# Moving pad fills from VectorE to GpSimd and GpSimd's own fills later, with new load order, tile order and PSUM rotation, in a gated mix of linear attention and a SwiGLU FFN

## The chip, the cores and the metric

The kernel runs on one core of one Trainium2 chip. The metric is the device time in microseconds (us) of a whole execution. Before the change it is 291.82 us (median of 4 runs, 291.61 to 292.34). Runs of one kernel scatter by up to 2.2 us here (291.45 to 293.68 for the kernel before on one chip; 3.0 us in e6, with one outlier), so experiments were run in five rounds beside the kernel before on the same chip, and comparisons between chips are made by the ratio to it.

Engines in the profile: PE = TensorE (matmuls), DVE = VectorE, ACT = ScalarE, POOL = GpSimd, SP = the queue that starts most DMAs; a q behind a name is the engine's own instruction queue. L330 is a line of the program, often a helper's: L340 fills, L330 `tensor_scalar`, L326 `scalar_tensor_tensor`, L322 `tensor_tensor`, L318 copies, L312 ScalarE's activations, L306 transposes, L294 matmuls. The granted clock is the share of its full clock that TensorE was given.

## The reference, cut to what matters

With S = 2048 tokens, D = 640, 32 heads of 20 and F = 1728:

```python
x = A_x
g = sigmoid((x * gate_w).sum(-1, keepdims=True))
q, k, v = split_heads(x @ A_wqkv)
# phi: softmax(+k @ w_phi) and softmax(-k @ w_phi), side by side
kv  = einsum("bhsf,bhsd->bhfd", phi_k, v);  z = phi_k.sum over tokens
a = (phi_q @ kv) / (phi_q . z + 1e-6)       # per head
b = (silu(x @ w_gate) * (x @ w_up)) @ w_down
out = g * (a @ wo) + (1 - g) * b
```

## The kernel before

The program is two lists of words. `LOADS` is the order of the DMAs, `ORDER` the order of the work items; each item sends its instructions to several engines, and every engine runs its own in that order. A helper counts who last wrote and read which bytes and places the waits. What matters here:

- `H` = two warming matmuls on ones, `X t` = transpose tile t of x on TensorE, `G` = the gate column, `U t.c` / `V t` = v projection of tile t, `M`/`R` = premultiply the k and q weights by w_phi, `K`/`S`/`P`/`E` = k tile, its sums, its normalisation on GpSimd (2.36 us each), its sum into k-v; `F b.k` = one FFN item; `Q`/`A`/`B`/`C`/`c` = the q side; `J` = the gates; `I`/`N` = begin and end of the k phase.
- PSUM is handed out in four pairs of banks. During the k phase pair 3 holds the k-v sums and the other three rotate.

```python
FCUT = [0, 384, 1024, F_FFN]                # three loads of gate/up columns
XQ = ["sp", "act", "act", "sp"]             # queues that load x0..x3
...
memset("dve", ones[:, :], 1.0)
for buf in (v1r, v1x):                      # pads of the v tiles
    v1v = buf[:, :, :].rearrange("p b (h d) -> p b h d", d=DH + 1)
    memset("dve", v1v[:, :, H, :], 0.0)
    memset("dve", v1v[:, :, :, DH:DH + 1], 1.0)
memset("dve", ekr[:, :, 1280:FK], 0.0)
memset("dve", krec[:, :, :], 0.0)
memset("pool", wog[:, :, :], 0.0)
...
memset("pool", ph[:, :, :], 0.0)            # 128 x 4224, buffers of the scaled q
...
def next_pair():
    r = ring["i"] % ring["n"]               # round robin; n is 3 in the k phase, else 4
    ring["i"] += 1
    return r
...
def kv_end():                               # N
    kv_finish()                             # VectorE: zt, zf, dz, then kvsb from banks 6 and 7
    ring["n"] = 4

def gates():                                # J, all on 128 x 16 float32
    tsc(svec[:, :], svec[:, :], 60.0, None, ALU.min, ALU.bypass)   # VectorE tensor_scalar
    actop(g2[:, :], svec[:, :], ACTF.Exp)                          # ScalarE
    tsc(omg[:, :], g2[:, :], 2.0, 2.0, ALU.mult, ALU.add)
    recip(omg[:, :], omg[:, :])
    tsc(g2[:, :], g2[:, :], 2.0, None, ALU.mult, ALU.bypass)

def fitem(bt, k):                           # F (cut)
    mm(...gate, up into the two banks of one pair...)
    actop(h, g, ACTF.Tanh, 0.5)             # ScalarE reads PSUM
    actop(u, up, ACTF.Copy)                 # ScalarE reads PSUM
    stt(h, h, 1.0, g, ALU.add, ALU.mult)    # VectorE reads PSUM: now the pair is free
    tt("pool", h, h, u, ALU.mult)           # GpSimd
```

The softmax here doesn't subtract the row's maximum and nothing guards it: scores larger than these inputs give would overflow.

## Time and profile before

| | before |
|---|---|
| span of the profiled execution | 289.8 us |
| PE busy | 285.8 us (99%) |
| DVE / ACT / POOL busy | 168.9 / 148.7 / 157.0 us |
| first useful matmul (transpose of x0) | 4.64 us |
| first gate matmul (F0.0) | 12.87 us |

The chain of waits of the kernel before (start, length, what; followed back from the last instruction) shows what bounds it:

```profile
3.66 0.33 DVE v1x L340
...
4.36 0.04 DVE wvg L318
...
4.45 0.39 PE ps L294 x2
...
11.49 276.34 PE ps L294 x1900
287.83 0.03 issue
287.86 0.32 DVE osb L697
```

After 11.49 us TensorE never stops: 1900 matmuls in one piece. The spacing is dense: a 128x512 matmul follows the last by 216 ns, from 12.87 us on, and the trace shows no closer spacing of that shape. So I saw nothing to win after the start without fewer matmuls, and much to lose: a wait put into that piece can cost up to its full length (an estimate from the piece without a stop).

The start in the timeline of before (start, length, engine, line, operation, output<-input, shapes, count; in brackets the idle time before it and what ended that):

```profile
2.85 0.82 PE L294 MATMUL ps<-ones 128*128 128x128 bf16 x6
...
3.66 0.33 DVE L340 MEMSET v1x<- 128x330 bf16 x1 [1.25 <-issue]
...
4.28 0.11 DVE L318 COPY wvg<-ps 128x5 bf16<-128x5 bf16 x1
...
4.45 0.39 PE L294 MATMUL ps<-ones 128*128 128x128 bf16 x2 [0.78 <-DVE wvg L318]
4.64 0.74 PE L306 MATMUL ps<-ident,xs 128*128 128x128 bf16 x5
```

The gate column's copy queues behind the pad fills on VectorE, and a warming matmul waits 0.78 us for its PSUM pair. That is what the change goes for.

The gates, from the same timeline:

```profile
75.05 0.17 DVE L330 TENSOR_SCALAR svec<-svec 128x16 f32<-128x16 f32 x1
75.21 1.15 POOL L322 TENSOR_TENSOR hT<-hT,us 128x512 bf16<-128x512 bf16 x1 [0.20 <-DVE svec L330]
...
75.50 0.89 DVE L330 TENSOR_SCALAR omg<-g 128x16 f32<-128x16 f32 x1 [0.28 <-ACT g L312]
...
76.59 0.11 DVE L330 TENSOR_SCALAR g<-g 128x16 f32<-128x16 f32 x1
```

Three `tensor_scalar` of the same 16 columns take 0.17, 0.89 and 0.11 us. The slow one ends at 76.39, just as GpSimd's product ends (75.21 + 1.15 = 76.36).

### The profile page before, as it was taken

The page shows a single profiled execution, that of the slowest core. Times are in us where ns is not written, and L with a number is a line of the kernel's source. Part 1 is how long each engine was busy: PE and PEld are TensorE (multiplying, and loading weights), DVE is VectorE, ACT ScalarE, POOL GpSimd, SP SyncE. Part 2 cuts the span into 40 slices and gives each one's busy share as a digit, 9 for nine tenths or more (in the row PEclk, how much of TensorE's full clock was granted, in tenths as well). Part 3 has the DMA queues.
Part 4 walks back from the last instruction along what each step waited for, and adds up shares of the span by engine and source line. Part 5 has one row for each costly group of instructions (what it writes and reads, how often), then busy time and mean ns, then how long its engine had stood idle before and what let it go on. Part 6 is the DMA issues. An engine that isn't in the chain of part 4 may idle for free.

```text
span 289.8 us, 4879 instructions
## 1 busy us (share of the span) xinstructions
PE 285.8 (99%) x1975; PEld 174.8 (60%) x1975; DVE 168.9 (58%) x248; ACT 148.7 (51%) x252; POOL 157.0 (54%) x118
## 2 busy tenths in 40 slices
PE   7999999999999999999999999999999999999997
PEld 5657777767544554447775557655444457746776
DVE  3244866768678999699998399238265337011000
ACT  1456778777465637584344743434565552172112
POOL 8731986987646786968333736411597454213000
PEclk9999999999999999999999999999999999999999
DMA  7976878000192205202362213500022003500101
GB/s 201 249 109 127 111 214 313 3 5 0 41 314 66 50 2 100 50 2 58 87 111 59 47 35 68 79 23 23 2 50 50 0 2 72 75 23 1 48 23 49
DMA packets 48777, 21.28 MB, mean 73 GB/s; under 512 B 39346, under 2 KB 48754, under 8 KB 48754
## 3 DMA queue, kind: packets, MB, share of 16 engines
q1 hardware_dynamic: 46712, 19.76, 31.1%
q10 hardware_dynamic: 2042, 1.20, 1.6%
q8 instruction: 16, 0.26, 0.4%
q14 instruction: 7, 0.06, 0.1%
HBM read 8.96 MB, written 2.62 MB: 40 GB/s over the span
## 4 chain that ended last, share of the span: by engine, by line
PE 98%; issue 1%; DVE 1%
PE ps L294 97%; PE ps L306 1%; DVE v1x L340 0%; DVE v1r L340 0%; DVE osb L697 0%; DVE krec L340 0%; DVE ones L340 0%; DVE ekr L340 0%; DVE wvg L318 0%
## 5 line engine op out<-in xcount | busy, mean ns | idle before, releaser
L322 POOL TENSOR_TENSOR hT<-hT,us 128x512 bf16<-128x512 bf16 (+1 forms) x56 | 67.5, 1215 | 67.9 <-DVE hT L326 67.7
L326 DVE SCALAR_TENSOR_TENSOR hT<-hT,ps 128x512 bf16<-128x512 bf16 (+1 forms) x56 | 37.8, 684 | 65.6 <-ACT hT L312 60.5
L294 PE MATMUL ps<-xT,wg 128*128 128x512 bf16 x260 | 64.6, 379 | 0.0
L294 PE MATMUL ps<-xT,wu 128*128 128x512 bf16 x260 | 64.6, 379 | 0.0
L294 PE MATMUL ps<-wd,hT 128*128 128x320 bf16 (+2 forms) x462 | 63.9, 295 | 0.0
L312 ACT ACTIVATE hT<-ps 128x512 bf16<-128x512 f32 (+2 forms) x60 | 35.8, 597 | 43.8 <-PE ps L294 43.6
L294 PEld LDWEIGHTS ps<-wd,hT 128*128 128x128 bf16 x462 | 44.5, 98 | 17.0
L322 POOL TENSOR_TENSOR ph<-eq,qc 128x1320 bf16<-128x1320 bf16 x16 | 40.3, 2520 | 24.8 <-DVE qc L610 15.3
L294 PE MATMUL ps<-wqk,xT 128*128 128x320 bf16 x320 | 47.7, 299 | 0.0
L312 ACT ACTIVATE osb<-ps,omg 128x640 bf16<-128x640 f32 (+2 forms) x17 | 12.9, 758 | 61.4 <-PE ps L294 61.4
L294 PEld LDWEIGHTS ps<-xT,wu 128*128 128x128 bf16 x260 | 25.4, 98 | 30.7
L322 POOL TENSOR_TENSOR ekr<-ekr,krec 128x1280 bf16<-128x1280 bf16 x16 | 37.4, 2357 | 11.5 <-DVE krec L336 9.6
L294 PEld LDWEIGHTS ps<-xT,wg 128*128 128x128 bf16 x260 | 24.9, 98 | 29.3 <-ACT oT L312 0.8
L294 PEld LDWEIGHTS ps<-wqk,xT 128*128 128x128 bf16 x320 | 30.7, 98 | 13.0 <-issue 0.4
L312 ACT ACTIVATE us<-ps 128x512 bf16<-128x512 f32 (+1 forms) x56 | 33.3, 595 | 1.3 <-POOL hT L322 1.2
L333 DVE TENSOR_REDUCE ksum<-ekr 128x64 f32<-128x1280 bf16 x16 | 23.4, 1464 | 12.4 <-ACT ekr L312 12.4
L312 ACT ACTIVATE eq<-ps 128x640 bf16<-128x640 f32 x32 | 22.4, 703 | 11.5 <-POOL ph L322 7.1
L312 ACT ACTIVATE ekr<-ps 128x640 bf16<-128x640 f32 x32 | 22.4, 704 | 7.2 <-PE ps L294 6.7
L333 DVE TENSOR_REDUCE qz<-eq 128x64 f32<-128x1280 bf16 x16 | 23.7, 1479 | 2.7 <-ACT eq L312 2.7
L294 PE MATMUL ps<-wvg,xT 128*128 128x320 bf16 (+1 forms) x160 | 25.0, 304 | 0.1
L294 PE MATMUL ps<-wog,oT 128*128 128x320 bf16 (+2 forms) x165 | 24.7, 294 | 0.0
L333 DVE TENSOR_REDUCE qw<-ez 128x64 f32<-128x1280 bf16 x16 | 23.6, 1478 | 0.1
(73 smaller groups left out, 191.6 us busy)
## 6 DMA issues: line engine op xcount, KB each, us to landing
out_dram<-osb SPq DMA_DIRECT2D x15, 160.0 KB, 1.8
wd<-in_B_w_down_dram SPq DMA_DIRECT2D x1, 2080.0 KB, 10.9
wg<-in_B_w_gate_dram SPq DMA_DIRECT2D x1, 880.0 KB, 9.8
wu<-in_B_w_up_dram SPq DMA_DIRECT2D x1, 880.0 KB, 11.5
wg<-in_B_w_gate_dram SPq DMA_DIRECT2D x1, 800.0 KB, 5.6
wu<-in_B_w_up_dram SPq DMA_DIRECT2D x1, 800.0 KB, 7.9
wog<-in_A_wo_dram SPq DMA_DIRECT2D x2, 375.0 KB, 7.5
wvg<-in_A_wqkv_dram SPq DMA_DIRECT2D x3, 160.0 KB, 4.1
```

The source lines that it names most:

```text
L294: last = pe.matmul(o, lhsT=l, rhs=r, start=st, stop=sp_, skip_group_check=sk)
L306: last = pe.transpose(o, i, ident[0:k, 0:k])
L312: return run("act", lambda: act.activation(o, i, func, scale=scale), rd, [o])
L322: return run(e, lambda: eo.tensor_tensor(o, a, b, op), [a, b], [o])
L326: return run("dve", lambda: dve.scalar_tensor_tensor(out=o, in0=a, scalar=s, in1=b, op0=op0, op1=op1), rd, [o])
L333: return run("dve", lambda: dve.tensor_reduce(o, i, AX.X, ALU.add), [i], [o])
```

## The change

The intent is to free VectorE at the start, to bring x2 and x3 sooner, to put less data ahead of the transposing DMAs, and to pick the PSUM pair whose last use lies furthest back. `LOADS` and `ORDER` are rewritten to fit.

```diff
-x0 w0 x1 w1 w2 x2 w3 w4 x3 f0 h k0 k1 t4 ...
+x0 w0 x1 w1 x2 w2 x3 w3 w4 h f0 k0 k1 t4 ...
-FCUT = [0, 384, 1024, F_FFN]
+FCUT = [0, 256, 896, F_FFN]
+XQ = ["sp", "act", "act", "act"]           (WQ alike, and the first up load on sp; cut)
 ORDER (cut to two places):
-H0 H3 H11 H8 H6 H7 H9 G H4 H5 H2 H1 X0 H10 X1 ...
+H0 H8 H6 H13 H9 H11 H5 H7 H10 G H2 H14 H12 H3 H1 X0 H4 X1 ...
-... P15 F1.6 J F0.12 E13 E14 E15 N L F0.7 ...
+... P15 i4 F1.13 F0.2 J F1.2 E12 E13 E14 E15 Q0 Q2 Q1 N F0.13 ...
+def fills(i):
+    if i < 2:      memset("pool", v pads of v1r / v1x)
+    elif i == 2:   memset("pool", ekr pads); memset("pool", krec)
+    elif i == 3:   memset("pool", wog), kvsb, eq, qc, hmask
+    else:          memset("pool", ph[:, :, :], 0.0)
+for i in range(3): fills(i)                 # i3 and i4 stand in ORDER
-ring = {"n": 4, "i": 0}
+ring = {"n": 4, "lru": [0, 1, 2, 3]}
+held = set()                                # pairs with an unfinished v tile
+def used(r): ...                            # puts pair r last in the order of use, returns it
 def next_pair():
-    r = ring["i"] % ring["n"]; ...
+    return used([r for r in ring["lru"] if r < ring["n"] and r not in held][0])
```

More of the change, by code (lines that the diff above doesn't have):

```diff
@@ L31 @@
 LOADS = """
-x0 w0 x1 w1 w2 x2 w3 w4 x3 f0 h k0 k1 t4 k2 k3 k4 t5 t6 t7 t8 t9 t10 t11 t12 t13 t14 t15 q0 q1 q2 q3
+x0 w0 x1 w1 x2 w2 x3 w3 w4 h f0 k0 k1 t4 k2 k3 k4 t5 t6 t7 t8 t9 t10 t11 t12 t13 t14 t15 q0 q1 q2 q3
 q4 f1 f2
@@ L36 @@
 ORDER = """
-H0 H3 H11 H8 H6 H7 H9 G H4 H5 H2 H1 X0 H10 X1 U0.0 U0.1 U1.0 U0.2 U1.1 X2 U1.2 U0.3 U1.3 U0.4 U2.0
-U2.1 U2.2 U1.4 X3 U2.3 U2.4 Y V3 F0.0 M0 F0.2 M1 F0.1 M3 M4 V4 M2 V5 K0 V8 S0 K1 S1 K2 K3 V7 V13
-P0 I S2 E0 K4 P1 E1 V6 S3 P2 P3 R1 S4 K5 V10 E2 K6 E3 P4 S5 E4 P5 S6 R0 K8 R3 K7 E5 P6 S7 K9 V9 S8
-E6 R4 V15 P7 S9 R2 K10 V14 E7 P8 P9 S10 K11 E8 V11 K12 P10 E9 S11 S12 P11 P12 K13 Q1 E10 K14 S13 T
-F0.3 E11 V12 A1 P13 K15 Q0 S14 S15 Q2 P14 E12 P15 F1.6 J F0.12 E13 E14 E15 N L F0.7 F1.12 F1.8 Z
-A0 B0 F0.11 C0 c0 B1 F0.13 F1.2 F0.9 F1.0 C1 F1.10 F0.5 A2 Q3 F1.13 B2 B3 c1 F0.4 Q4 A3 C2 c2
-F0.10 F1.4 C3 Q5 c3 B5 F1.11 F0.8 A5 F1.5 F0.6 F1.1 F1.7 A4 F1.9 B4 C4 c4 O0.1 Q6 O0.0 C5 c5 A6
-O0.2 F1.3 Q7 B6 B7 D0.3 A7 D0.0 Q8 C6 c6 C7 c7 Q9 A9 D0.2 Q10 B9 B8 D0.1 A8 C8 O1.0 O1.1 c8 A10 C9
-O1.2 F2.11 Q11 c9 F2.5 B10 Q12 A12 F2.6 C10 B11 F2.4 A11 F2.10 D1.1 C11 c10 Q13 B12 D1.0 A13 c11
-F2.13 B13 Q14 D1.3 F2.7 C13 F2.1 C12 D1.2 O2.2 B14 A14 O2.0 O2.1 F3.10 F3.0 c13 F3.4 F2.12 F3.13
-c12 F3.9 C14 F3.8 F2.8 F3.1 F3.7 F2.2 F3.6 F2.3 F2.9 F3.2 F2.0 F3.12 Q15 c14 A15 D2.1 B15 C15 c15
-D2.2 D2.3 O3.2 O3.1 O3.0 F3.3 F3.11 F3.5 D2.0 D3.2 D3.1 D3.0 D3.3
+H0 H8 H6 H13 H9 H11 H5 H7 H10 G H2 H14 H12 H3 H1 X0 H4 X1 U0.0 U0.1 U1.0 X2 U1.1 U0.2 U1.2 U2.0
+U2.1 X3 U2.2 U1.3 Y U2.3 U1.4 U0.3 U2.4 V3 U0.4 i3 F0.0 F0.1 M0 M1 V4 M2 M3 M4 K0 S0 K1 K3 S1 P0
+P1 K2 V5 V6 I E0 K4 S2 P2 S3 V8 E1 K5 E2 V7 K6 P3 E3 S4 S5 K7 V11 P4 P5 E4 V14 S6 P6 K8 E5 R0 S7
+K9 V9 S8 R1 P7 E6 S9 E7 P8 K10 R3 K11 P9 S10 E8 V10 V13 E9 R4 K12 S11 P10 K13 T E10 K14 S12 P11
+P12 E11 S13 V12 V15 S14 R2 K15 P14 P13 F1.10 S15 F0.11 P15 i4 F1.13 F0.2 J F1.2 E12 E13 E14 E15 Q0
+Q2 Q1 N F0.13 A0 F1.11 Z B0 F0.7 B1 F1.7 C0 c0 F0.6 F1.3 A1 A2 F0.3 L B2 C1 F0.5 Q3 c1 B3 F0.10
+F1.0 Q4 C2 c2 B4 F0.12 F1.12 F0.4 A3 F1.1 C3 Q5 B5 c3 F0.8 A5 F1.5 F1.8 F0.9 A4 F1.4 F1.9 C5 c5 C4
+O0.2 Q6 c4 O0.1 O0.0 A6 B6 Q7 Q8 C6 B7 D0.2 A7 D0.1 c6 A8 C7 c7 Q9 D0.0 A9 Q10 B8 C8 F1.6 D0.3 B9
+O1.0 O1.2 B10 C9 O1.1 F2.6 c9 c8 F2.2 D1.0 Q12 Q11 A10 C10 F2.8 c10 Q13 A11 F2.7 F2.13 A13 B11
+D1.3 C11 F2.10 c11 D1.2 F2.4 B12 B13 A12 D1.1 O2.1 O2.0 O2.2 C12 Q14 C13 F2.11 c12 F2.1 F3.6 Q15
+F2.12 F2.0 A15 F2.9 B15 c13 F2.5 F3.8 F2.3 F3.13 C15 F3.5 c15 F3.7 B14 F3.11 F3.1 F3.9 F3.12 A14
+F3.0 C14 F3.4 F3.10 D2.1 c14 F3.3 D2.3 O3.2 O3.0 O3.1 F3.2 D2.0 D2.2 D3.0 D3.1 D3.2 D3.3
 """
@@ L356, in select @@
             channel_multiplier=cm), [ap], [ap])
-    XQ = ["sp", "act", "act", "sp"]
-    WQ = ["sp", "sp", "act", "sp", "act"]
+    XQ = ["sp", "act", "act", "act"]
+    WQ = ["sp", "sp", "sp", "sp", "act"]
     x2 = A_x[0]
@@ L374, in load_ffn @@
         dma("sp", wg[:, :, c0:c1], B_w_gate[:, c0:c1].rearrange("(c p) j -> p c j", p=P))
-        dma("sp" if c0 else "act", wu[:, :, c0:c1], B_w_up[:, c0:c1].rearrange("(c p) j -> p c j", p=P))
+        dma("sp", wu[:, :, c0:c1], B_w_up[:, c0:c1].rearrange("(c p) j -> p c j", p=P))
     def load_wv(c):
@@ L402, in _build @@
     memset("dve", ones[:, :], 1.0)
-    for buf in (v1r, v1x):
-        v1v = buf[:, :, :].rearrange("p b (h d) -> p b h d", d=DH + 1)
-        memset("dve", v1v[:, :, H, :], 0.0)
-        memset("dve", v1v[:, :, :, DH:DH + 1], 1.0)
-    memset("dve", ekr[:, :, 1280:FK], 0.0)
-    memset("dve", krec[:, :, :], 0.0)
-    memset("pool", wog[:, :, :], 0.0)
-    memset("pool", kvsb[:, :, :], 0.0)
-    memset("pool", eq[:, :, 1280:FP], 0.0)
-    memset("pool", qc[:, :, :], 0.0)
-    memset("pool", ph[:, :, :], 0.0)
-    memset("pool", hmask[:, :], 1.0)
-    select(hmask[:, :], [[-40, 3]], ALU.is_ge, 0.0, 0, 1)
-    select(hmask[:, :], [[40, 3]], ALU.is_gt, 0.0, 40, -1)
+    def fills(i):
+        if i < 2:
+            v1v = (v1r, v1x)[i][:, :, :].rearrange("p b (h d) -> p b h d", d=DH + 1)
+            memset("pool", v1v[:, :, H, :], 0.0)
+            memset("pool", v1v[:, :, :, DH:DH + 1], 1.0)
+        elif i == 2:
+            memset("pool", ekr[:, :, 1280:FK], 0.0)
+            memset("pool", krec[:, :, :], 0.0)
+        elif i == 3:
+            memset("pool", wog[:, :, :], 0.0)
+            memset("pool", kvsb[:, :, :], 0.0)
+            memset("pool", eq[:, :, 1280:FP], 0.0)
+            memset("pool", qc[:, :, :], 0.0)
+            memset("pool", hmask[:, :], 1.0)
+            select(hmask[:, :], [[-40, 3]], ALU.is_ge, 0.0, 0, 1)
+            select(hmask[:, :], [[40, 3]], ALU.is_gt, 0.0, 40, -1)
+        else:
+            memset("pool", ph[:, :, :], 0.0)
+    for i in range(3):
+        fills(i)
     def load_late_weights():
@@ L428, in tail_weights, with used @@
         copy("pool", wt[:, :, 64:P], wu[:, :, 13 * P:F_FFN])
-    ring = {"n": 4, "i": 0}
+    ring = {"n": 4, "lru": [0, 1, 2, 3]}
+    held = set()
+    def used(r):
+        ring["lru"].remove(r)
+        ring["lru"].append(r)
+        return r
     def next_pair():
-        r = ring["i"] % ring["n"]
-        ring["i"] += 1
-        return r
+        return used([r for r in ring["lru"] if r < ring["n"] and r not in held][0])
     def xpose(t):
@@ L476, in vpart @@
             vpr[t] = next_pair()
+            held.add(vpr[t])
         mm(v_pairs(t, vpr[t])[2 * c:2 * c + 2])
         if c == 4:
+            held.remove(used(vpr[t]))
             v_out(t, vpr[t])
@@ L711, in _build @@
     ops = {
-        "H": lambda i: warm(), "X": xpose, "G": gcol, "U": vpart, "V": vtile,
+        "H": lambda i: warm(), "i": fills, "X": xpose, "G": gcol, "U": vpart, "V": vtile,
         "M": lambda m: premult(1, m), "R": lambda m: premult(0, m),
```

## The prediction

> **What bounds the kernel now.** TensorE. The chain of waits is 97.2% one line of matmuls, and after 11.49 us it is one piece of 276.34 us without a stop. In the timeline a 128x512 matmul follows the last by 216 ns, a 128x320 one by 136 ns; I found only 0.6 us lost after 12.9 us (around 20.0 us). VectorE (58%), ScalarE (51%) and GpSimd (54%) have slack on average. The matmuls do not change, so nearly all that can be won lies in the first 21 us:
> - 4.64 us before the first useful matmul (transpose of x0);
> - of those, 0.78 us idle (3.67 to 4.45; list of waits): a warming matmul waits for the PSUM pair of the gate column, whose VectorE copy (4.28) queues behind the fills of the v pads (the last at 3.66);
> - about 1.3 us because the array runs at half speed until about 6.5 us (128-column matmuls follow each other by 107 to 116 ns, later 55). [...];
> - 0.3 us at 10.7 us, 0.6 us at 20.0 us.
>
> **What the change does.** Four pad fills (0.16 to 0.33 us each) and two others leave VectorE; the gate copy should come near 3.1 us and the 0.78 us gap go. On GpSimd they add about 1.5 us, while 4.4 us of fills (`wog` 2.76, `kvsb` 0.68, small ones) move behind the block weights and 3.6 us (`ph`) to the end of the k phase, where GpSimd has 2.36 us per k tile against about 3.1 us of TensorE. Three more warming pairs (0.64 us cold) put the first transpose at about 4.2 us, without a gap before it. x2 and x3 come sooner. The first gate/up load falls from 960 to 640 KB: 0.3 MB less at the 290 GB/s seen there is about 1.1 us earlier for the transposing DMAs, less one more issue (0.45 us) ahead of them. The cost: two FFN items, not three, cover the wait for the k weights.
>
> **On the critical path.** Start 0.4 us earlier; head waits 0.3 to 0.5; the stall at 20.0 us perhaps 0.5. [...] For new small stalls (k weights, PSUM pairs, a late GpSimd) I take off 0.3 us. Net gain about 1.3 us; ceiling about 3 us.
>
> **Prediction.** 290.3 us; 8 in 10 between 289.0 and 292.0. Faster by over 2%: 0.01; within 2%: 0.95; slower by over 2%: 0.04.
>
> **What the profile would show.** Right: gate copy before 3.5 us, no gap between warming matmuls; first transpose at 4.0 to 4.4 us; first gate matmul about 12.0 us instead of 12.87; first k tile near 19 to 20 us instead of 23.67 (order, not gain); no wait of TensorE over 0.5 us afterwards; tail after the last matmul unchanged. Wrong: TensorE idle before the premultiplication of the k weights or the k tiles (transposing DMAs still late), matmuls waiting for ScalarE or VectorE to free a PSUM pair in the denser k phase or in the q phase (VectorE is already 90 to 98% busy between 100 and 160 us), or fills on GpSimd delaying the normalised k tiles.
>
> **What would make it wrong.** [...] The order after 25 us is all new; one ill-fitted dependence there can cost several us. The three runs of before span 0.7 us, half of the gain.

Three passages on when and why TensorE's clock rises are cut from this text, because no run here shows them; one was a term of the sum, a gain of up to 1 us or nothing. The terms left (0.4, 0.3 to 0.5, 0.5, less 0.3) come to 0.9 to 1.1 us; with the cut term the sum was about 1.3. The half speed that the text names is read from the spacing alone: the granted clock of before is 1.00 from the start. Its "0.64 us cold" is six matmuls at the 107 ns measured there.

## The result, and the profile after

The changed kernel takes 295.06 us (median of 4, 294.25 to 295.65): 1.0107 times before, interval 1.0078 to 1.0135. It is slower by about 1%, outside the predicted range.

| | before | after |
|---|---|---|
| span of the profiled execution | 289.8 us | 293.9 us |
| first useful matmul | 4.64 us | 4.31 us |
| first gate matmul | 12.87 us | 12.35 us |
| from there to the end of the span | 276.9 us | 281.6 us |

The last row (span less first gate matmul) places the loss: the start has gained, and 4.6 us (281.55 - 276.93) are lost later. The chain of waits of the changed kernel says where:

```profile
9.22 60.83 PE ps L294 x551
...
70.07 0.60 ACT hT L312
...
70.70 0.69 DVE hT L326
71.38 4.28 DVE svec L330
...
75.68 0.23 ACT g L312
...
81.83 210.07 PE ps L294 x1279
```

The single dense piece is now broken between 70 and 82 us, and the longest link there is a VectorE instruction on 16 columns. The start, in the timeline of the changed kernel, went as predicted:

```profile
3.27 1.25 PE L294 MATMUL ps<-ones 128*128 128x128 bf16 x10
3.38 0.18 DVE L318 COPY wvg<-ps 128x5 bf16<-128x5 bf16 x1 [2.31 <-PE ps L306]
...
4.31 0.74 PE L306 MATMUL ps<-ident,xs 128*128 128x128 bf16 x5
```

The copy comes at 3.38 and no warming matmul waits. The gates, in the same timeline:

```profile
69.71 2.36 POOL L322 TENSOR_TENSOR ekr<-ekr,krec 128x1280 bf16<-128x1280 bf16 x1
...
71.30 4.35 DVE L330 TENSOR_SCALAR svec<-svec 128x16 f32<-128x16 f32 x1
72.00 3.62 POOL L340 MEMSET ph<- 128x4224 bf16 x1
...
73.41 2.88 PE L294 MATMUL ps<-wqk,xT 128*128 128x320 bf16 x20
...
75.68 0.22 ACT L312 ACTIVATE g<-svec 128x16 f32<-128x16 f32 x1 [4.53 <-DVE svec L330]
...
77.78 0.68 DVE L326 SCALAR_TENSOR_TENSOR hT<-hT,ps 128x512 bf16<-128x512 bf16 x1
...
78.52 2.71 PE L294 MATMUL ps<-wqk,xT 128*128 128x320 bf16 x10 [2.23 <-DVE hT L326]
...
81.83 1.37 PE L294 MATMUL ps<-xT,wt 128*128 128x512 bf16 x5 [0.60 <-DVE kvsb L322]
```

Read it from the top. The `tensor_scalar` on `svec`, 0.17 us before, starts in the profile at 71.30 while GpSimd still multiplies a k tile, and ends at 75.65, within 0.03 us of the end of the fill of `ph` (72.00 + 3.62 = 75.62). It starts 0.70 us before the fill and yet ends with it; why the fill went first is not shown. ScalarE's `g` waits 4.53 us for it; behind `g` stands the evacuation of F1.2; VectorE's part of that comes at 77.78; only then is a PSUM pair free, and the third q tile has waited 2.23 us. The next FFN item waits 0.60 us more for VectorE to read the k-v sums. The list of waits of TensorE agrees:

```profile
PE ps L294 <- DVE hT L326: 2.2, 1, 2.2
PE ps L294 <- DVE ones L340: 1.1, 1, 1.1
PE ps L294 <- DVE kvsb L322: 0.6, 1, 0.6
```

(Total, times, longest.) The waits after the start add up to 2.8 us, less than was lost: the three q tiles take 81.83 - 73.41 = 8.42 us, where 30 matmuls at 136 ns are 4.08. Of the missing 4.34 us, 2.8 are waits, and the rest is mostly the array's clock, 0.50 for most of that tile: after the pause the third q tile needs 2.71 us for 10 matmuls, 1.52 elsewhere (69.75 us in before). The windows of the changed kernel (stretch in us, its length, busy time of PE, PEld, DVE, ACT, POOL with counts, then the granted clock, DMA share, GB/s):

```profile
76.40:78.50 2.10, 0.00 (x0) 0.00 (x0) 2.07 (x6) 2.07 (x4) 1.43 (x2) 1.00 0.00 0
78.50:79.20 0.70, 0.69 (x4) 0.41 (x5) 0.63 (x4) 0.67 (x2) 0.66 (x1) 0.64 0.00 0
79.20:79.80 0.60, 0.60 (x4) 0.36 (x3) 0.60 (x1) 0.33 (x1) 0.49 (x1) 0.50 0.00 0
```

The granted clock falls to half at about 78.7 us, 0.2 us after work resumes, and is full again from 82.1 us. This costs some 1.3 us in the profiled run (2.71 - 1.53 in the third q tile, 1.37 - 1.24 in the five matmuls after it). It is not the whole story: that run's mean granted clock is 0.994, but the three other runs of the changed kernel have 1.000 and are as slow (294.25 to 295.65). They have no profile, so what they lost in its place is not shown.

**Theory A.** The fill of `ph`, moved to just ahead of the gates, holds up VectorE's `tensor_scalar` for as long as the fill runs. In its narrow form: only a form with one SBUF input is held by a fill, which reads nothing; a form with two is held only while GpSimd runs an instruction that reads, such as the k multiply. So far this is a conjecture, suggested by the two end times (75.65 and 75.62); nothing up to here tells the forms apart.
**Theory B.** The new order is to blame: three q tiles right behind the last k tiles, three rotating pairs.
**Theory C.** Handing out pairs by last use is to blame: pair 3, set aside in the k phase, is then the one used longest ago, so it is handed out first although VectorE still has to read it.

### The profile page after: what moved, and what is told of

Same layout as the page of the kernel before. It is cut to its first block, busy times and chain, and to the rows that moved or that the text cites. A ratio compares the mean times of both kernels' runs of the same rounds, so it can differ in the third digit from the quotient of the medians. Undisturbed runs are those within 1.5% of the kernel's fastest.

```text
span 293.9 us, 4887 instructions
## 1 busy us (share of the span) xinstructions
PE 287.9 (98%) x1981; PEld 175.9 (60%) x1981; DVE 171.6 (58%) x242; ACT 147.9 (50%) x252; POOL 160.1 (54%) x124
## 4 chain that ended last, share of the span: by engine, by line
PE 95%; DVE 4%; ACT 0%; issue 0%
PE ps L294 94%; DVE svec L330 1%; DVE dz L322 1%; PE ps L306 1%; DVE hT L326 0%; DVE omg L330 0%; DVE g L330 0%; DVE kvsb L322 0%; ACT hT L312 0%; DVE osb L712 0%; DVE omg L336 0%; ACT g L312 0%; DVE zf L333 0%; DVE zt L322 0%; DVE ones L340 0%
## 5 line engine op out<-in xcount | busy, mean ns | idle before, releaser
L294 PE MATMUL ps<-wqk,xT 128*128 128x320 bf16 x320 | 48.8, 304 | 2.2 <-DVE hT L326 2.2
```

What stands on the lines that cost most here:

```text
L294: last = pe.matmul(o, lhsT=l, rhs=r, start=st, stop=sp_, skip_group_check=sk)
```

## The experiments

### e1: the fill of `ph` back at the start

```diff
-    for i in range(3):
+    for i in (0, 1, 2, 4):
         fills(i)
-... P15 i4 F1.13 F0.2 J ...
+... P15 F1.13 F0.2 J ...
```

> The changed kernel with one thing moved: the fill of ph goes back to the head of GpSimd's program. Theory A ([...] the gate chain, the evacuation of F1.2 and then TensorE wait): the tensor_scalar on svec takes under 1 us instead of 4.35, TensorE's stop between 73.4 and 81.8 us (4.3 us lost) shrinks to under 0.7 us, time 290.3 to 291.5 us. Theory B (the new order with three q tiles behind the last k tiles, three PSUM pairs and last-use pairs is to blame, the fill is not): stop stays over 3 us, time 294 to 295.5 us.

Measured: 290.88 us (six runs), ratio 0.9966 (0.9950 to 0.9983), faster than before. `svec` took 0.79 us. TensorE has one wait left there, 0.64 us. The timeline of e1:

```profile
70.85 0.79 DVE L330 TENSOR_SCALAR svec<-svec 128x16 f32<-128x16 f32 x1
...
77.84 1.25 PE L294 MATMUL ps<-xT,wt 128*128 128x512 bf16 x5 [0.64 <-DVE kvsb L322]
```

The order and the pairs are the changed kernel's, so B cannot explain most of the loss, and A's main figure is met. From the first gate matmul (11.90) to the end of the span (289.8) it is 277.9 us: 3.6 of the 4.6 us are back.

### e2: two-input forms of the gates, the fill left late

```diff
-tsc(svec, svec, 60.0, None, ALU.min, ALU.bypass)
+tt("dve", svec, svec, c60, ALU.min)               # c60: a tile of 60
-tsc(omg, g2, 2.0, 2.0, ALU.mult, ALU.add)
+stt(omg, g2, 2.0, c2, ALU.mult, ALU.add)          # c2: a tile of 2
-tsc(g2, g2, 2.0, None, ALU.mult, ALU.bypass)
+tt("dve", g2, g2, g2, ALU.add)
```

> The changed kernel with the fill of ph left late; only the three small VectorE tensor_scalar of the gates are written with two SBUF inputs (minimum with a tile of 60, scalar_tensor_tensor with a tile of 2, sum with itself). [...] they run during the fill: svec at most 1 us (the tail of the k multiply before the fill), the others under 0.3 us, stop of TensorE under 1 us, time 290.5 to 291.8. If any VectorE work on SBUF waits for a GpSimd fill, or the order is to blame (B): svec over 3 us or stop over 3 us, time 294 to 295.5.

(The cut condition is theory A in its narrow form, with a cause that no run here shows.)

Measured: 289.99 us (289.89 to 290.18), ratio 0.9935 (0.9921 to 0.9949), the fastest and below the expected range. The timeline of e2 (its L324 is `tensor_tensor`, L328 `scalar_tensor_tensor`, L342 the fill):

```profile
70.64 0.79 DVE L324 TENSOR_TENSOR svec<-svec,c 128x16 f32<-128x16 f32 x1
71.35 3.62 POOL L342 MEMSET ph<- 128x4224 bf16 x1
...
71.72 0.18 DVE L328 SCALAR_TENSOR_TENSOR omg<-g,c 128x16 f32<-128x16 f32 x1 [0.28 <-ACT g L314]
...
72.10 0.11 DVE L324 TENSOR_TENSOR g<-g 128x16 f32<-128x16 f32 x1
...
72.75 4.24 PE L296 MATMUL ps<-wqk,xT 128*128 128x320 bf16 x30
...
76.82 1.24 PE L296 MATMUL ps<-xT,wt 128*128 128x512 bf16 x5
```

The fill is where it was, and both later instructions run during it, in 0.18 and 0.11 us. `svec` ends at 71.43, with the k multiply, which reads (69.05 + 2.36 = 71.41). The three q tiles take 4.07 us (76.82 - 72.75) where the changed kernel took 8.42. From the first gate matmul (11.70) to the end of the span (288.6) it is 276.9 us, as in before.

### e3: before, with the fill of `ph` late

```diff
-    memset("pool", ph[:, :, :], 0.0)           # at the start
-... P15 F1.6 J ...
+... P15 i4 F1.6 J ...                          # i4: the same fill
```

> The kernel before with one thing moved: the fill of ph goes from the head to just behind the last k multiply, ahead of the gates. Theory A: the tensor_scalar on svec, 0.17 us before, takes about 3.5 us; TensorE stops for 1 to 3.5 us near 77 to 84 us; time 293 to 295.2. Theory B: 291.4 to 292.3, svec stays under 1 us.

Measured: 293.68 us, ratio 1.0062 (1.0040 to 1.0083). The timeline of e3:

```profile
75.61 3.62 POOL L340 MEMSET ph<- 128x4224 bf16 x1
75.71 3.55 DVE L330 TENSOR_SCALAR svec<-svec 128x16 f32<-128x16 f32 x1
...
81.41 0.81 PE L294 MATMUL ps<-xT,wg 128*128 128x512 bf16 x3 [1.62 <-DVE zt L322]
```

The fill alone produces the stall in the old order, with the old pairs. It costs 1.6 us there instead of 4.6. That FFN items rather than three q tiles follow the gates is the likely reason; it was not tested.

### e4 and e5: before with pairs by last use; then with pair 3 put last

e4 is the kernel before with the new `next_pair`, `used` and `held`, nothing else. e5 adds one line:

```diff
     def kv_end():
         kv_finish()
         ring["n"] = 4
+        used(3)                # the pair of the k-v sums goes last
```

> The kernel before with nothing but PSUM pairs by last use. If the pairs matter to the loss: over 292.5 us. Theory A says they do not: within 0.4 us of before (291.4 to 292.2), no stop of TensorE over 0.5 us.

> The kernel before with pairs by last use (298.8 us in the earlier run), and the pair that holds the k-v sums put last in the order of use when the k phase ends. Theory C (last use hands out just that pair first, since no other tile used it in the k phase, and the next FFN item then waits for VectorE to read the sums): the wait for the kvsb reads (4.1 us) and the half-speed matmuls after it vanish, time within 0.5 us of before: 291.5 to 292.5. Rival (any other shift of pairs is to blame): 294 us or more.

Measured: e4 298.79 us, ratio 1.0241 (1.0215 to 1.0266), against my expectation of no effect. e5 292.20 us, ratio 1.0008 (0.9986 to 1.0031): all of it gone. The timeline of e4:

```profile
76.89 1.20 PE L294 MATMUL ps<-v1x,ekr 128*128 128x63 bf16 x33
82.16 2.31 PE L294 MATMUL ps<-xT,wg 128*128 128x512 bf16 x5 [4.08 <-DVE kvsb L322]
84.26 2.34 PE L294 MATMUL ps<-xT,wu 128*128 128x512 bf16 x5
86.40 2.09 PE L294 MATMUL ps<-xT,wg 128*128 128x512 bf16 x5
```

Theory C is real: the FFN item behind `N` gets the pair of the k-v sums and waits 4.08 us for their readers, and then the array runs at half speed (granted clock 0.50, five matmuls in 2.1 us instead of 1.08) for some 6 us. So last use is not harmless; the changed order mostly hides it, because three q tiles stand between the last k-v sum and `N`.

### e10: the changed kernel with only pair 3 put last

The edit is the line of e5, on the changed kernel.

> The changed kernel with only the k-v pair put last in the order of use at the end of the k phase; late fill and gates as changed. Theory C on top of A: the wait of F0.13 for the kvsb reads (0.6 us[...]) goes, the wait of the third q tile for the pair of F1.2 (2.2 us) stays: 293.3 to 294.6 us. If the last-use pairs were the larger part of the loss (as 6.7 us in the kernel before suggest): under 292 us.

Measured: 293.50 us, ratio 1.0038 (1.0003 to 1.0073). In its profile the 0.6 us wait is gone and the 2.23 us wait of the third q tile is not:

```profile
77.86 1.53 PE L294 MATMUL ps<-wqk,xT 128*128 128x320 bf16 x10 [2.23 <-DVE hT L326]
```

So C's share in the changed kernel is the smaller one. By the ratios (1.0038 against 1.0107, other rounds) e10 is still some 2 us faster than the changed kernel, more than that wait of 0.6 us; how the rest divides between pair, clock and start is not shown. The six runs fall into two groups, 292.39 to 292.70 and 294.31 to 294.44. The profiled run is the 292.39 one, and there the third q tile kept the full clock after its wait (granted clock 1.00, 1.53 us for 10 matmuls). The record has the mean granted clock of every run: 1.000 in the first group and 0.994 in the second, as in the changed kernel's profiled run. So the second group had less than the full clock for a while; at which place is not seen, as these runs have no profile.

### e9: the late fill cut to the pads

```diff
-memset("pool", ph[:, :, :], 0.0)                                   # 4224 columns
+memset("pool", ph.rearrange("p b (j c) -> p (b j) c", c=P)[:, :, 120:P], 0.0)   # 264
```

> The changed kernel with the late fill of ph kept in its place but limited to the 8 pad columns of each 128 (264 elements for 4224, all that the program needs zero); gates as changed. Theory A says that VectorE is held exactly as long as GpSimd's instruction runs: fill about 0.3 us, tensor_scalar on svec about 0.8 to 1.2 us (rest of the k multiply plus the fill), TensorE's stop under 1 us, 290.6 to 291.4 us. If the place of the fill rather than its length did it (an instruction more between k multiply and FFN product): over 293 us.

Measured: 291.24 us, ratio 0.9959 (0.9932 to 0.9987). The timeline of e9:

```profile
69.50 2.36 POOL L322 TENSOR_TENSOR ekr<-ekr,krec 128x1280 bf16<-128x1280 bf16 x1
...
71.10 1.05 DVE L330 TENSOR_SCALAR svec<-svec 128x16 f32<-128x16 f32 x1
71.81 0.31 POOL L340 MEMSET ph<- 128x264 bf16 x1
```

`svec` ends at 72.15, again at the end of the fill (72.12), not at the end of the k multiply ahead of it (69.50 + 2.36 = 71.86). Place and count of instructions are unchanged; the hold is shorter with the shorter fill (`svec` 1.05 us with a fill of 0.31, 4.35 with one of 3.62).

### e6: all three cures together

The early fill of e1, the two-input gates of e2 and the line of e5.

> The changed kernel with the three cures together: fill of ph at the head, gates in two-input forms, the k-v pair last in the order of use. If each cure only removes a wait in the 70 to 82 us stretch, and two-input gates alone left no wait there, nothing more is to be won: 289.6 to 290.3 us, the same as with two-input gates alone (289.99). If the late fill still cost something elsewhere, below 289.5.

Measured: 290.21 us (one of six runs at 293.00), ratio 0.9951 (0.9919 to 0.9983): the same as e2. With the fill out of the way GpSimd now multiplies FFN tiles, which reads, while the two-input gates run: `g` ends at 76.63, the second product at 76.59 (74.33 + 2.26). From the timeline of e6:

```profile
74.33 2.26 POOL L324 TENSOR_TENSOR hT<-hT,us 64x512 bf16<-64x512 bf16 x2
...
74.69 0.89 DVE L328 SCALAR_TENSOR_TENSOR omg<-g,c 128x16 f32<-128x16 f32 x1 [0.28 <-ACT g L314]
...
75.78 0.85 DVE L324 TENSOR_TENSOR g<-g 128x16 f32<-128x16 f32 x1
```

The same two instructions took 0.18 and 0.11 us in e2 under the fill. So the late fill is, with two-input gates, even a little better for VectorE than FFN products in its place. The profile is of the 293.00 run: a chunk of wv landed late there (TensorE waited 0.8 us at 7.1 us) and the first gate matmul came at 14.67 us.

### e7, e8, e11: the start

Three variants of e2. e7 puts the pad fills back on VectorE. e8 goes back to the old order, queues and sizes of the first loads. e11 moves work ahead of the last warming matmuls:

```diff
 e7  -memset("pool", v1v[...])  +memset("dve", v1v[...])       (ekr and krec alike)
 e8  LOADS, XQ, WQ, FCUT and the queue of the first up load as before the change
 e11 -G H2 H14 H12 H3 H1 X0 H4 X1 U0.0 U0.1
     +G X0 H2 H14 H12 H3 U0.0 H1 X1 H4 U0.1
```

> The kernel with two-input gates (289.99 us), with the fills of the v pads, ekr and krec back on VectorE as before the change. If these fills are what cost at the head: gate column copy at about 4.3 us, a gap of 0.4 to 0.8 us among the warming matmuls, first gate matmul at 12.3 to 13.5 us instead of 11.7, time 290.6 to 291.8. If they are harmless: 289.8 to 290.2.

> The kernel with two-input gates (289.99 us), with the order, the queues and the sizes of the first loads as before the change (384 columns of gate/up first). If the smaller and later first load matters: TensorE waits 0.5 to 1.5 us for transposed k weights or k tiles between 16 and 24 us, or for x2/x3 before 10 us, time 290.5 to 291.5. If not: 289.8 to 290.3.

> A try at a better version: two-input gates, and the transposes of x0 and the first v matmuls moved ahead of the last warming matmuls. If the count of warming matmuls ahead of x0 sets the start: first v matmul near 4.9 us instead of 5.64, first gate matmul 0.3 to 0.7 us earlier, 289.3 to 289.8 us. If the loads of x1 and w1 set it: 289.8 to 290.2 us.

| run | time, us | ratio to before | first gate matmul |
|---|---|---|---|
| e2 | 289.99 | 0.9935 (0.9921 to 0.9949) | 11.70 |
| e7 pads on VectorE | 290.61 | 0.9948 (0.9929 to 0.9966) | 12.43 |
| e8 old loads | 291.58 | 0.9971 (0.9948 to 0.9994) | 13.42 |
| e11 early x0 | 290.64 | 0.9944 (0.9914 to 0.9974) | 11.79 |

In e7 a warming matmul waits 0.41 us for the gate column's copy, as it did in before; about 0.6 us by the medians, but the intervals of e2 and e7 overlap (different chips), so the size is uncertain. In e8 TensorE waits 0.46 us for x2, and stops another 0.42 us before the first gate matmul; the medians differ by 1.6 us, and the intervals all but part. e11 gained nothing and lies above both ranges expected: the first v matmuls came at 4.76 us, but one of the next waited 0.20 us for VectorE's copy of the transposed x1, and the first gate matmul stayed where it was. So the warming matmuls ahead of x0 do not set the start here; their number was not varied.

## Why the prediction was wrong

- **What bounds the kernel: right.** TensorE, dense after the start, so gains only in the start. In e2 the part behind the first gate matmul is 276.9 us as in before.
- **The start: right in mechanism, too small in size.** Predicted and found: copy of the gate column before 3.5 us (3.38), no gap between warming matmuls, first transpose at 4.0 to 4.4 us (4.31), first gate matmul about 12.0 us (12.35; 11.70 to 12.15 in e1, e2, e9 and e10), first k tile at 19 to 20 us (19.70). The net gain without the stall was put at 1.3 us; e2 shows 292.13 - 289.99 = 2.1 us. The fills took GpSimd some 3.5 us (3.68 to 7.14) instead of the 1.5 us put down for them, and TensorE waited for none of them. The matmuls came closer together about as before: five 128-column transposes take 0.74 us at 5.06 and 0.44 us at 7.12 (in before 0.74 at 5.38 and 0.44 at 7.91). The granted clock reads 1.00 all this time, so why they speed up is not shown. The profile of before was a lucky sample: with the same start, e3, e4 and e5 had their first gate matmul at 13.53, 13.98 and 13.80 us instead of 12.87.
- **0.6 us "lost at 20.0 us": a misreading.** I took the rest of a merged row for a pause. The 12 matmuls there take 0.63 us, 52 ns each. There was nothing to win.
- **The step that failed**: "For new small stalls (k weights, PSUM pairs, a late GpSimd) I take off 0.3 us", and the sentence on which it rests, that the fill of `ph` moves "to the end of the k phase, where GpSimd has 2.36 us per k tile against about 3.1 us of TensorE". I costed the fill in GpSimd's own time and found slack there. That slack was real: nobody waited for GpSimd's results in this stretch. What the fill cost was VectorE's time: `svec` took 4.35 us, against 0.17 before and 0.79 in the changed order without the late fill (e1). Through it TensorE lost 3.6 of the 4.6 us (281.55 - 277.9), the half clock of the profiled run included. Shown by taking the fill away (e1), by shortening it (e9), by forms that run during it in 0.18 and 0.11 us (e2), and by putting it into the kernel before (e3).
- **PSUM pairs**: named as a risk, not examined. The flaw in last use (e4, 6.7 us in the old order; e5 cures it) costs 0.6 us of waiting in the changed order (0.64 in e1, 0.90 in e9), probably because the q tiles ahead of `N` cover the rest.
- The sum: 2.1 us won at the start, about 5.1 us lost (295.06 - 289.99, medians of different rounds) make the measured loss of about 3 us; both are read from these same medians, so this is no check. The profile places 4.6 us behind the first gate matmul.

Still open is where the runs of the changed kernel without a profile, at full clock, lost their 5.1 us, and the exact size of the gain by the pads alone.

## What to carry to other kernels

A fill moved to an engine with slack is not free: here a fill of 3.62 us on GpSimd, with the k multiply before it, stretched a one-input VectorE instruction from 0.17 to 4.35 us, and this shows in the profile as a long VectorE instruction, not as a wait. When a tiny instruction takes several times longer in one place than in another, look at what the other engine finishes at that moment. And when buffers are handed out by last use, one that was set aside is the oldest, and comes out first just when its readers are still to come.

## What the runs showed of the hardware

- A two-input form was stretched while GpSimd multiplied, which reads (0.89 and 0.85 us in e6), and not during its fill (0.18 and 0.11 us in e2). A `tensor_scalar` was stretched by both: 0.89 us beside a product of 1.15 us in before, 3.55 us beside the fill of 3.62 us in e3. In the changed kernel the fill and the k multiply before it stretched an instruction of 0.17 us to 4.35 us and cost most of 4.6 us of TensorE. Rewriting one-input forms with two inputs, or filling only the pads (0.31 us), is a cure. What the two engines contend for is not shown.
- The slice of `svec` contains the whole hold: 71.30 to 75.65 us in the changed kernel, ending 0.03 us after the fill. The time lost to it therefore counts as busy time of VectorE and is in no list of VectorE's waits there.
- In the profiled run of the changed kernel the granted clock fell to 0.50 at about 78.7 us, 0.2 us after a pause of 2.23 us had ended, while the profiled run of e10 kept 1.00 after a pause of the same length. In e4 it fell about 3.2 us into the pause of 4.08 us (estimated from its mean of 0.90 between 78.0 and 82.1 us, if it fell straight to 0.50). So the same pause came with a lower clock in one run and not in another; what decides it is not shown.
